# Both chunk pairs of a spatial mixing by one Strassen level, on eight fixed PSUM banks

## The chip, the core and the metric

The kernel runs on one core of a Trainium2 chip. The metric is the device time of one execution in microseconds, the median of several runs. TensorE (PE) does the matmuls, VectorE (DVE) and ScalarE (ACT) the elementwise work, GpSimd (POOL) a little of it. DMA transfers are started from the queues of SyncE (SP) and of ACT.

## The reference

```
xn = layernorm(x)                                  # x: 2048 x 512
# A: attention of 32 heads of width 16; each row sees itself and 7 earlier rows, 2 apart
q, k, v = split(xn @ wqkv)
s = softmax_window(q, k) @ v, then @ wo            # 512 x 512
# B: gated MLP with a mixing over the rows
z  = gelu(xn @ w_in)                               # 2048 x 1792
z1 = z[:, :896]
z2 = layernorm(z[:, 896:])
g  = w_sp @ z2 + b_sp[:, None]                     # w_sp: 2048 x 2048: the spatial mixing
return x + s * silu((z1 * g) @ w_out)              # w_out: 896 x 512
```

Everything is float32. The change is in the line of `g`.

## The kernel before

Every float32 operand of a matmul is written as the sum of a rounded high part and the rest. The helper `split` (L185, L186) makes them: ACT writes the high part, DVE subtracts it from the source and writes the low part. A product is then three matmuls (high x high, high x low, low x high), done by the helper `three` (L765 to L769, the line L767 in the profile). `prep` fetches a 128 x 512 block of weights by a DMA on SP's queue into one of four raw buffers and splits it into one of eight weight pairs.

The work goes through these stages on PE: `xn` and the product with `wqkv`; z1 (line L650 to L652), 7 blocks of 128 columns, kept transposed, gated later and until then in device memory (`z1_d`); z2 (L678 to L680), 16 row tiles in pairs (i, i + 8), then normalised and split into the large buffer `BIG`; the mixing (L767); the projection with `w_out` (tile `b`, L982 to L984); the product with `wo` (tile `s`, the same lines) and the end. The attention itself is DVE work with a share of POOL. It is emitted before z1 at the lowest priority and fills DVE from the z1 stage on; its results (`o_d`) are read by the product with `wo`.

The mixing forms g transposed: 7 column blocks f of z2, four chunks c of 512 rows each of the output, 16 row tiles s (8 upper, 8 lower) to sum over. z2 is the stationary operand, a 128 x 512 block of `w_sp` the moving one. Chunks 2 and 3 go plainly, one after the other: for each of 16 row tiles all 7 column blocks, in 7 PSUM banks. Chunks 0 and 1 go together by one level of Strassen's scheme over chunk (0 or 1), half of the rows (upper or lower) and half of the columns (f = 0 to 2, or 4 to 6; f = 3 is the odd column and goes plainly): seven products of 3 column blocks and 8 row tiles take the place of eight. The combinations that it needs are made ahead: `block_sums` loads two pairs of `w_sp` blocks, adds them in four DVE instructions (L639) and stores two 512 KB tiles to `sums_d`; `combine` (L712) does the same for z2 after its normalisation and stores to `t_d`. During the mixing `operand` loads those back (tile `tr`, L824) and splits them into parts of `BIG` that no product needs any more. `block_product` runs a product in four steps of two row tiles, and after each step does what its `steps` list says.

Results are multiplied with z1. Those of chunks 2 and 3 are stored to `g_d`, and loaded and split again by `late` when there is room in `BIG` (table `slots`); those of chunks 0 and 1 are split at once by `gated`.

Most temporary tiles of these stages are the eight wide buffers of the tag `t4` (128 x 1024): the z1 tiles before they are stored, the raw z2 tiles, the tiles of `block_sums` (`sa`, `sb`), the operands, the biases, the results between products. A tile takes a free buffer and holds it until its last reader is done.

The order of the instructions on each engine and of the DMA issues on SP and ACT is fixed when the kernel is built: a scheduler goes through the instructions by priority (program order, unless a priority is set by `urgent` or the attention's low one) and puts those first that are ready by its own estimate of time. The engines then work each in that order.

Of the kernel before, what the change touches and what calls it, by code (L numbers as in the profile page):

```python
# [57 lines left out]
def kernel(  # L58
# [67 lines left out]
    slots = {(0, f): f for f in range(4)}  # L126
    slots.update({(2, f): 4 + f for f in range(5)})
    slots.update({(1, f): 5 + f for f in range(4, FB)})
    slots.update({(2, 5): 12, (2, 6): 13, (0, 4): 18, (0, 5): 19, (0, 6): 22})
    slots.update({(3, 0): 23, (3, 1): 26, (3, 2): 27, (1, 0): 14, (1, 1): 15, (1, 2): 16, (1, 3): 17})  # L130
    slots.update({(3, 3): 20, (3, 4): 21, (3, 5): 24, (3, 6): 25})
# [497 lines left out]
    def block_sums(i):  # L629
        top, low = t4(f"sa_{i}"), t4(f"sb_{i}")  # L630
        nc.sync.dma_start(top, w_sp[0:2, i].rearrange("c p t -> p c t"))
        nc.sync.dma_start(low, w_sp[0:2, HT + i].rearrange("c p t -> p c t"))
        for out_, a, b in (
            (low[:, 1], top[:, 1], low[:, 1]),
            (top[:, 1], top[:, 0], top[:, 1]),
            (top[:, 0], top[:, 0], low[:, 1]),
            (low[:, 0], top[:, 0], low[:, 0]),
        ):
            nc.vector.tensor_tensor(out_, a, b, op=ALU.add)  # L639
        nc.scalar.dma_start(sums_d[0, i], top)  # L640
        nc.scalar.dma_start(sums_d[1, i], low)

    for f in range(FB):
# [18 lines left out]
        if f % 2:  # L662
            block_sums(f // 2)
# [33 lines left out]
    def z2_normal(j, zt):  # L697
# [6 lines left out]
    def combine(i, zts):  # L704
        b11, b12, b21, b22 = [z[:, p_] for z in zts for p_ in (first_part, last_part)]
        for out_, a, b, op in (
            (b11, b11, b12, ALU.subtract),
            (b12, b22, b12, ALU.subtract),
            (b22, b22, b11, ALU.add),
            (b21, b22, b21, ALU.subtract),  # L710
        ):
            nc.vector.tensor_tensor(out_, a, b, op=op)  # L712
        for a, zt in enumerate(zts):
            v = zt[:, first_part]
            src = bass.AP(
                tensor=v.tensor, offset=v.offset, ap=[list(v.ap[0]), [FH - F3, 2], [1, F3]]
            )
            nc.scalar.dma_start(t_d[a, i], src)

    early_pair = [wts.tile([P, CT], F32R, tag=f"w{n}", name=f"wsp_2_0{n}") for n in "hl"]  # L720
    split(*early_pair, fetch(w_sp[2, 0], CT, "wsp_2_0"))
    spatial = {(2, 0): early_pair}
    raw_z = {}
    for i in range(HT + 2):
        if i < HT:
            raw_z[i] = [t4(f"zt_{j}").rearrange("p i t -> p (i t)")[:, :FH] for j in (i, HT + i)]
            for h in range(2):
                for j, zt in zip((i, HT + i), raw_z[i]):
                    z2_half(j, h, zt)
                if i == HT - 1 and h == 0:  # L730
                    spatial[2, HT] = spatial_block(2, HT)
# [3 lines left out]
        if i > 1:  # L735
            for j, zt in zip((i - 2, HT + i - 2), raw_z[i - 2]):
                z2_normal(j, zt)
            combine(i - 2, raw_z[i - 2])

    def bias(c):  # L740
        t = t4(f"bb_{c}")
        nc.sync.dma_start(
            t, b_sp[c : c + 2, :].rearrange("c t -> (c t)").unsqueeze(0).to_broadcast([P, 2 * CT])
        )
        return t

    def load_o(g, k, i=None):
# [7 lines left out]
        else:  # L755
            oh, ol = half(2 * i), half(2 * i + 1)
# [22 lines left out]
    order = [i + h * HT for i in range(HT) for h in range(2)]  # L779
    bb = bias(2)  # L780
    banks = {(2, f): mm(f"g_2_{f}") for f in range(FB)}
    seeds = set()

    def seed(key, name, src, scale=1.0):
        banks[key] = mm(name)
        nc.scalar.activation(banks[key], src, AF.Copy, scale=scale)
        seeds.add(key)

    for c in (2, 3):
        for n, js in enumerate(order):  # L790
            w = spatial.get((c, js)) or spatial_block(c, js)
            for f in range(FB):
                key = c, f
                three(banks[key], z2_block(js, f), w, n == 0 and key not in seeds, n == NT - 1, key in seeds)
            if n == HT:
                if c == 2:
                    banks[3, 0] = mm("g_3_0")
                else:
                    b01 = bias(0)
                    seed(("p", 0), "p1_0", b01[:, 0])  # L800
            if c == 2 and n % 4 == 0 or c == 3 and n == 5:
                block_sums(3 + n // 4 if c == 2 else 7)
        for f0 in range(0, FB, 2):
            n = min(2, FB - f0)
            zl = z1_pair(c, f0, n)
            gts = None if (c, f0 + n - 1) in seeds and f0 else t4(f"gt_{c}_{f0}", n)
            for f in range(f0, f0 + n):
                zt, src = zl[:, f - f0], banks[c, f]
                if (c, f) not in seeds:
                    gt = gts[:, f - f0]  # L810
                    nc.vector.tensor_tensor(gt, src, bb[:, c - 2], op=ALU.add)
                    src = gt
                nc.vector.tensor_tensor(zt, src, zt, op=ALU.mult)
                if c == 2 and f < FB - 1:
                    seed((3, f + 1), f"g_3_{f + 1}", bb[:, 1])
                if c == 3 and f < 3:
                    key = ("p", f + 1) if f < 2 else ("o", 0)
                    seed(key, f"p1_{f + 1}", b01[:, 0])
            nc.scalar.dma_start(g_d[c - 2, f0 : f0 + n].rearrange("f p t -> p f t"), zl)

    def operand(i, half_, s0):
        raw = t4(f"tr_{half_}{i}_{s0}").rearrange("p i t -> p (i t)")[:, : 2 * F3]
        rv = raw.rearrange("p (j f t) -> p j f t", j=2, f=3)
        nc.sync.dma_start(  # L824
            rv, t_d[half_, s0 : s0 + 2, :, i].rearrange("j p (f t) -> p j f t", t=P)
        )
        hi, lo = [
            planes[:, FB - 3 :, s0 : s0 + 2, a].rearrange("p f j t -> p j f t") for a in range(2)
# [3 lines left out]
    def block_product(name, key, z, w, odd=None, start=True, steps=()):  # L832
        for n, s0 in enumerate(range(0, HT, 2)):
            pair_ = [(s, prep(w(s), CT, f"{name}_{s}")) for s in (s0, s0 + 1)]
            for f in range(3):
                for s, wp in pair_:
                    three(
                        banks[key, f], z(s, f), wp, start and s == 0, s == HT - 1, not start
                    )
            if odd:  # L840
                for s, wp in pair_:
                    three(banks["o", odd[0]], odd[1](s), wp, False, s == HT - 1, True)
            for do in steps[n] if steps else ():
                do()

    def upper(s, f):
        return z2_block(s, f)
# [240 lines left out]
```

## Time and profile before

| | |
|---|---|
| median of 3 runs | 708.12 us (708.11 to 708.29) |
| profiled execution | 708.39 us, span 706.6 us |
| PE busy | 700.8 us, 99% of the span |
| DVE busy | 586.4 us, 83% |
| ACT busy | 268.3 us, 38% |
| POOL busy | 112.6 us, 16% |
| DMA traffic | 159.29 MB, 225 GB/s in the mean |
| mixing on PE | 294.7 to 583.0 us |

The page of the profile shows one execution. A group of instructions is told by line, engine, operation and tiles; behind the bar stand its busy time, the mean duration of one in ns, the idle time of the engine just before them and what ended it. Matmuls overlap in the pipeline, so that the mean duration of one, some 390 ns, is longer than the distance to the next.

### The profile page before, as it was taken

What the parts mean: (1) busy time and instruction counts of PE and PEld (TensorE: products, weight loads), DVE (VectorE), ACT (ScalarE), POOL (GpSimd) and SP (SyncE); (2) the same over time, 40 slices, a digit from 0 to 9 for tenths busy, and PEclk for the clock granted to TensorE, in tenths of its full rate; (3) what the DMA queues carried; (4) which work ended last, traced back from release to release, by engine and by line L of the source; (5) the groups of instructions that cost most, each with busy time, mean ns of one, the idle gap of its engine ahead of it and who ended that gap; (6) DMA issues with size and microseconds to landing.
All of it is one profiled execution on the core that took longest, in us unless ns stands there. A gap on an engine that the chain in (4) does not pass through costs nothing.

```text
span 706.6 us, 9137 instructions
## 1 busy us (share of the span) xinstructions
PE 700.8 (99%) x3152; PEld 585.6 (83%) x3152; DVE 586.4 (83%) x845; ACT 268.3 (38%) x417; POOL 112.6 (16%) x110
## 2 busy tenths in 40 slices
PE   8999999999999999999999999999999999999997
PEld 7888888888888988888888888888888888888886
DVE  6774479999999899998999999999999989330464
ACT  4343332334442666662113111344545452131621
POOL 3100002211212344540121112111101100000000
PEclk9999999999999999999999999999999999999999
DMA  8768677778798132498969745878868682273785
GB/s 269 258 186 244 173 247 208 197 258 301 264 330 263 50 108 97 140 309 298 384 203 336 245 138 162 286 253 291 276 202 275 202 290 94 78 219 153 246 251 232
DMA packets 100110, 159.29 MB, mean 225 GB/s; under 512 B 9056, under 2 KB 51296, under 8 KB 100064
## 3 DMA queue, kind: packets, MB, share of 16 engines
q1 hardware_dynamic: 61424, 116.11, 51.1%
q10 hardware_dynamic: 38640, 42.60, 17.4%
q8 instruction: 24, 0.39, 0.2%
q14 instruction: 22, 0.18, 0.1%
HBM read 107.74 MB, written 50.94 MB: 225 GB/s over the span
## 4 chain that ended last, share of the span: by engine, by line
PE 98%; DMA 1%; DVE 1%; SPq 0%; issue 0%
PE g L767 22%; PE q L767 12%; PE p L767 6%; PE qkv L373 6%; PE qkv L375 6%; PE qkv L374 6%; PE z L680 4%; PE z L679 4%; PE z L678 4%; PE z L652 4%; PE b L983 4%; PE z L650 4%; PE b L984 4%; PE b L982 4%; PE z L651 4%; PE s L983 2%
## 5 line engine op out<-in xcount | busy, mean ns | idle before, releaser
L571 POOL TENSOR_TENSOR pv<-pv 128x1024 f32<-128x1024 f32 x29 | 69.8, 2406 | 377.1 <-DVE pv L561 377.0
L517 DVE TENSOR_TENSOR pr<-k,q 128x2048 f32<-128x2048 f32 x32 | 73.2, 2287 | 6.6 <-DMA q<-qkv_d 4.6
L561 DVE TENSOR_TENSOR pv<-v,lg 128x2048 f32<-128x2048 f32 x32 | 73.2, 2288 | 0.6
L524 DVE TENSOR_REDUCE lg<-pr 128x128 f32<-128x2048 f32 x32 | 72.9, 2277 | 0.0
L390 ACT ACTIVATE stage<-qkv 128x512 f32<-128x512 f32 x36 | 21.5, 596 | 47.6 <-PE qkv L375 47.6
L993 ACT ACTIVATE bt<-b 128x512 f32<-128x512 f32 x16 | 9.5, 597 | 45.6 <-PE b L984 45.6
L699 ACT ACTIVATE zt<-zt,nmz,mvz 128x896 f32<-128x896 f32 x16 | 17.8, 1134 | 20.8 <-POOL nmz L695 20.8
L680 PE MATMUL z<-w_0h,BIG 128*128 128x512 f32 x64 | 25.0, 391 | 0.0
L679 PE MATMUL z<-w_0l,BIG 128*128 128x512 f32 x64 | 25.0, 391 | 0.0
L678 PE MATMUL z<-w_0h,BIG 128*128 128x512 f32 x64 | 24.9, 389 | 0.0
L186 DVE TENSOR_TENSOR o_1l<-ol,o_1h 128x512 fp32r<-128x512 f32 x3 | 2.1, 689 | 26.7 <-ACT o_1h L185 26.7
L1037 DVE TENSOR_TENSOR sg<-s,sg 128x512 f32<-128x512 f32 (+1 forms) x17 | 11.2, 659 | 15.1 <-PE s L984 15.0
L269 DVE TENSOR_TENSOR xT<-xT,mr 128x512 f32<-128x512 f32 x20 | 13.7, 687 | 11.3 <-DMA mr<-mv_d 6.7
L576 DVE TENSOR_TENSOR pv<-pv 128x512 f32<-128x512 f32 x32 | 21.8, 682 | 0.1
L680 PE MATMUL z<-w_1h,BIG 128*128 128x384 f32 x64 | 21.5, 336 | 0.0
L678 PE MATMUL z<-w_1h,BIG 128*128 128x384 f32 x64 | 21.5, 335 | 0.0
L679 PE MATMUL z<-w_1l,BIG 128*128 128x384 f32 x64 | 21.4, 335 | 0.0
L690 DVE BATCH_NORM_STATS2 zst<-zt 128x6 f32<-128x448 f32 x32 | 18.8, 605 | 2.4 <-ACT zt L681 2.2
L659 ACT ACTIVATE z1t<-z 128x512 f32<-128x512 f32 x21 | 12.4, 593 | 20.2 <-PE z L652 17.1
L186 DVE TENSOR_TENSOR BIG<-zt,BIG 128x896 fp32r<-128x896 f32 x16 | 17.3, 1089 | 0.6 <-ACT BIG L185 0.4
L375 PE MATMUL qkv<-wqkv_0h,BIG 128*128 128x512 f32 x43 | 16.7, 389 | 0.0
L373 PE MATMUL qkv<-wqkv_1h,BIG 128*128 128x512 f32 x43 | 16.7, 389 | 0.0
(543 smaller groups left out, 2185.0 us busy)
## 6 DMA issues: line engine op xcount, KB each, us to landing
qkv_d<-stage ACTq DMA_DIRECT2D x24, 512.0 KB
k<-qkv_d SPq DMA_DIRECT2D x16, 704.0 KB
v<-qkv_d SPq DMA_DIRECT2D x16, 704.0 KB
z_d<-z1t ACTq DMA_DIRECT2D x14, 512.0 KB
t_d<-zt ACTq DMA_DIRECT2D x16, 384.0 KB
zl<-z_d SPq DMA_DIRECT2D x12, 512.0 KB
tr<-t_d SPq DMA_DIRECT2D x16, 384.0 KB
x<-in_x SPq DMA_DIRECT2D x16, 256.0 KB
```

The lines of the kernel that those rows point to most:

```text
L373: nc.tensor.matmul(pq, xh[:, k], wh, start=k == 0, stop=False)
L374: nc.tensor.matmul(pq, xh[:, k], wl, start=False, stop=False)
L375: nc.tensor.matmul(pq, xl[:, k], wh, start=False, stop=k == KB - 1)
L517: line(nc.vector.tensor_tensor(pr, taps(ks[u], j0), qb.unsqueeze(1).to_broadcast([P, W, NJ * CS]), op=ALU.mult))
L524: line(nc.vector.tensor_reduce(lgs[u][:, :, j0 * HS : (j0 + NJ) * HS], pr.rearrange("p w (i d) -> p w i d", d=DH), axis=AX.X, op=ALU.add,))
L561: line(nc.vector.tensor_tensor(pv.rearrange("p w (i d) -> p w i d", d=DH), taps(vs[u], j0).rearrange("p w (i d) -> p w i d", d=DH), lgs[u] ...
L571: eng.tensor_tensor(pv[:, 0:4], pv[:, 0:4], pv[:, 4:8], op=ALU.add)
L678: nc.tensor.matmul(pz, xh[:, k], wh, start=k == 0, stop=False)
L679: nc.tensor.matmul(pz, xh[:, k], wl, start=False, stop=False)
L680: nc.tensor.matmul(pz, xl[:, k], wh, start=False, stop=k == KB - 1)
L767: nc.tensor.matmul(pg, z[a], w[b], start=start and i == 0, stop=stop and i == 2, skip_group_check=seeded)
L983: nc.tensor.matmul(pp[:, cols], hi, wl, start=False, stop=False)
```

## The change

Chunks 2 and 3 go by the same scheme as chunks 0 and 1. The two pairs are called a = 0 (chunks 0 and 1) and a = 1 (chunks 2 and 3). The products of the pairs alternate: m1, m2, m6, m7, m4, m5, m3, each for a = 0 and then for a = 1. Each pair has four fixed PSUM banks, three for the column blocks of the running product and one for the odd column. They are allocated once; ACT writes a bias or an earlier product into them (`seed`) where the next product is to be added to it. The banks of the second pair are first written by four matmuls with the first weights, and then seeded (`second_seeds`).

`block_sums` is done for both pairs: seven blocks of the first pair in the z1 stage (three before), the eighth and all eight of the second pair in the first two products of the mixing. The first product of each pair is copied out of PSUM and stored to `x_d` (`kept`), to be loaded and subtracted later (`stored_gates`); the sum after the third product goes to `y_d` (`spill`) and is loaded by `upper_last`. `combine` forms its differences with the other sign, and one of the four results is split at once into `BIG`, so that three are stored, not four. Only the first four results of chunks 0 and 2 go through `g_d`. The order of the chunks in the projection with `w_out` is 1, 3, 0, 2 instead of 2, 0, 3, 1, and in the product with `wo` 1, 3, 0, 2 instead of 0, 2, 3, 1.

```diff
-    g_d = dram.tile([2, FB, P, CT], F32, name="g_d")
-    sums_d = dram.tile([2, HT, P, 2, CT], F32, name="sums_d")
-    t_d = dram.tile([2, HT, P, 2, F3], F32, name="t_d")
+    g_d = dram.tile([2, ODD + 1, P, CT], F32, name="g_d")
+    x_d = dram.tile([2, ODD, P, CT], F32, name="x_d")
+    y_d = dram.tile([2, ODD, P, CT], F32, name="y_d")
+    sums_d = dram.tile([2, 2, HT, P, 2, CT], F32, name="sums_d")
+    t_d = dram.tile([3, HT, P, F3], F32, name="t_d")
...
-        if f % 2:
-            block_sums(f // 2)
+        block_sums(0, f)
...
-        split(zh, zl, blocks(zt, FB))
+        split(zh[:, :n], zl[:, :n], blocks(zt, FB)[:, :n])
...
+        split(*[t[:, ODD + 1 :] for t in z2_at(i)], blocks(b22, ODD))
...
+        nc.scalar.dma_start(t_d[:2, i].rearrange("a p t -> p a t"), src)
+        nc.scalar.dma_start(t_d[2, i], b21)
...
+    b_a = t4("b_a")
+    nc.sync.dma_start(
+        b_a, b_sp[0:2, :].rearrange("c t -> (c t)").unsqueeze(0).to_broadcast([P, 2 * CT])
+    )
+    biases = [[b_a[:, 0], b_a[:, 1]]]
...
-    for c in (2, 3):
-        for n, js in enumerate(order):
-            w = spatial.get((c, js)) or spatial_block(c, js)
-            for f in range(FB):
-                key = c, f
-                three(banks[key], z2_block(js, f), w, n == 0 and key not in seeds, n == NT - 1, key in seeds)
...
+    banks = {}
+    for n in range(8):
+        a, f = n // 2 % 2, n // 4 * 2 + n % 2
+        banks[a, f] = mm(f"g_{a}_{f}")
+
+    def seed(a, f, src, scale=1.0):
+        nc.scalar.activation(banks[a, f], src, AF.Copy, scale=scale)
+
+    def evict(a, f, out_):
+        nc.scalar.activation(out_, banks[a, f], AF.Copy)
+
+    def block_product(a, name, z, w, odd=None, start=False, stop=False, steps=()):
+        for n, s0 in enumerate(range(0, HT, 2)):
+            pair_ = [(s, w(s)) for s in (s0, s0 + 1)]
+            for f in range(ODD):
+                for s, wp in pair_:
+                    three(banks[a, f], z(s, f), wp, start and s == 0, s == HT - 1, not start)
+            if odd:
+                for s, wp in pair_:
+                    three(banks[a, ODD], odd(s), wp, False, s == HT - 1, True)
+            for do in steps[n] if steps else ():
+                do()
...
+    def stored_gates(a, f0):
+        zl = z1_pair(2 * a, f0, 2)
+        n = min(2, ODD - f0)
+        xl = t4(f"xl_{a}_{f0}", n)
+        nc.sync.dma_start(xl, x_d[a, f0 : f0 + n].rearrange("f p t -> p f t"))
...
+            times(zl[:, f - f0], banks[a, f], zl[:, f - f0])
+            if f < ODD:
+                seed(a, f, xl[:, f - f0], -1.0)
+        nc.scalar.dma_start(g_d[a, f0 : f0 + 2].rearrange("f p t -> p f t"), zl)
...
+    def spill(a):
+        ta, tb = t4(f"ya_{a}"), t4(f"yb_{a}", 1)
+        for f in range(ODD):
+            y = ta[:, f] if f < 2 else tb[:, 0]
+            evict(a, f, y)
+            nc.vector.tensor_tensor(banks[a, f], banks[a, f], biases[a][1], op=ALU.add)
...
+        seed(a, ODD, biases[a][1])
...
+    def second_seeds():
+        biases.append([wts.tile([P, CT], F32, tag=f"w{n}", name=f"b_b{n}") for n in "hl"])
...
+            nc.tensor.matmul(
+                banks[1, f], z2_block(0, 0)[0], early_pair[0], start=True, stop=True
+            )
+        for f in range(ODD + 1):
+            seed(1, f, biases[1][0])
...
+        0, "m1a", at(0, 0), plain(0, 0, 0), odd(0),
+        steps=([second_seeds, sums(0, 7)], [sums(1, 0)], [sums(1, 1)], [sums(1, 2)]),
...
+        1, "m1b", at(0, 0), plain(1, 0, 0), odd(0),
+        steps=([sums(1, 3)], [sums(1, 4)], [sums(1, 5), sums(1, 6)], [sums(1, 7)]),
...
+    kept(1)
...
+        0, "m2a", at(1, 0), plain(0, 0, 1), odd(1),
...
+    block_product(1, "m2b", at(1, 0), plain(1, 0, 1), odd(1))
...
+        0, "m6a", at(0, LAST), summed(0, 0, 0), steps=([T4[0]], [T4[1]], [T4[2]], [T4[3]])
...
+    spill(0)
+    block_product(1, "m6b", at(0, LAST), summed(1, 0, 0))
+    spill(1)
```

The products m7 (with the odd column), m4 (with the odd column), m5 and m3 follow in the same manner. `summed` reads its weights from `sums_d`, `plain` from `w_sp`.

More of the change, by code (lines that the diff above doesn't have):

```diff
@@ L755, in load_o @@
         else:
[L756 removed]
+            oh, ol = i
         arrived[g] = split(
@@ L827, in operand @@
         hi, lo = [
-            planes[:, FB - 3 :, s0 : s0 + 2, a].rearrange("p f j t -> p j f t") for a in range(2)
+            planes[:, f0 : f0 + ODD, r0 + s0 : r0 + s0 + 2, b].rearrange("p f j t -> p j f t")
+            for b in range(2)
         ]
         split(hi, lo, rv)
[L832 to L844, printed above, removed]
@@ new lines, in upper_last, with sums @@
+    def upper_last(a, f0, n):
+        zl, yl = z1_pair(2 * a, LAST + f0, n), t4(f"yl_{a}_{f0}", n)
+        nc.sync.dma_start(yl, y_d[a, f0 : f0 + n].rearrange("f p t -> p f t"))
+        for f in range(f0, f0 + n):
+            minus(yl[:, f - f0], banks[a, f], yl[:, f - f0])
+            gated(2 * a, LAST + f, yl[:, f - f0], zl[:, f - f0])
+    T1, T3, T4 = [[later(operand, i, s0) for s0 in range(0, HT, 2)] for i in range(3)]
+    def sums(a, i):
+        return later(block_sums, a, i)
+    with urgent(300):
+        for f in range(ODD + 1):
+            seed(0, f, biases[0][0])
@@ L977, in proj @@
+    wout = [prep(w_out[:, f, :], D, f"wout_{f}") for f in range(FB)]
+    upper_last(1, 0, 2)
+    upper_last(1, 2, 1)
+    for a in range(2):
+        late(a, 0, 2)
+        late(a, 2, 1)
     def proj(n, src, w, name, cols=slice(0, D)):
```

303 lines of the change are left out of this document (126 added, 177 removed).

## The prediction

> **What bounds the kernel now.** I read the page first: the busy shares (busy us, share of the span, instructions) and the chain that ended last.
>
> ```profile
> PE 700.8 (99%) x3152; PEld 585.6 (83%) x3152; DVE 586.4 (83%) x845; ACT 268.3 (38%) x417; POOL 112.6 (16%) x110
> PE 98%; DMA 1%; DVE 1%; SPq 0%; issue 0%
> ```
>
> PE is the bound: nothing but fewer PE instructions can shorten this, and every wait that PE gets is paid in full. Then the chain in order of time (start, length, what), for the mixing, and PE's timeline at the two ends of what follows it.
>
> ```profile
> 294.83 152.36 PE g L767 x672
> 447.19 43.52 PE p L767 x192
> 490.71 20.40 PE q L767 x90
> ...
> 581.83 1.36 PE o L767 x6
> ```
> ```profile
> 583.03 0.39 PE L982 MATMUL b<-wout_0h,BIG 128*128 128x512 f32 x1
> ...
> 659.19 0.39 PE L982 MATMUL s<-BIG 128*128 128x512 f32 x1
> ```
>
> The plain pair is 672 matmuls in 152.36 us without a gap, 0.2267 us each. All the mixing, 672 + 600 = 1272 matmuls, is 288.4 us, from 294.7 to 583.03; then the projection b (336 matmuls, 76.2 us) and, from 659.19, s.
>
> Last, windows: what the other engines have to spare. Columns: stretch, its length, busy us of each engine, granted clock, share of DMA time, GB/s.
>
> ```profile
> 141.30:217.40 76.10, 76.10 (x338) 63.00 (x337) 74.11 (x93) 30.89 (x48) 15.03 (x7) 1.00 0.84 282
> 217.40:294.80 77.40, 77.40 (x386) 69.62 (x385) 74.60 (x117) 47.39 (x66) 33.43 (x52) 1.00 0.37 119
> 294.80:403.00 108.20, 108.20 (x479) 89.56 (x478) 105.17 (x159) 30.68 (x47) 22.48 (x22) 1.00 0.86 296
> 583.20:659.40 76.20, 76.20 (x337) 63.09 (x337) 30.44 (x43) 20.91 (x34) 0.00 (x0) 1.00 0.38 130
> 335.00:340.00 5.00, 5.00 (x23) 4.14 (x23) 3.82 (x6) 2.04 (x3) 0.00 (x0) 1.00 1.05 402
> 350.00:355.00 5.00, 5.00 (x23) 4.13 (x22) 4.96 (x9) 0.63 (x1) 0.00 (x0) 1.00 1.02 404
> 105.00:603.00 498.00, 498.00 (x2242) 417.84 (x2241) 484.38 (x676) 199.08 (x308) 102.64 (x93) 1.00 0.70 230
> ```
>
> DVE is full from 105 to 603 us (484.38 of 498.00), because the attention fills what the rest leaves. The DMA is at 0.86 in the first 108 us of the mixing; where its share is full it moves 402 to 404 GB/s. Between them lies the risk.
>
> **PE's share of the change.** A Strassen pair is seven products of 72 matmuls plus 24 for the odd column in four of them: 600 instead of 672. The second pair saves 72; four opening matmuls of the second pair's banks are added. Net 68 x 0.2267 = 15.4 us. Alternating the pairs moves matmuls and adds none.
>
> **DVE.** Its instructions follow each other closer than their durations say; starts give the pitch.
>
> ```profile
> 560.08 0.69 DVE L186 TENSOR_TENSOR q_3l<-q_3r,q_3h 128x512 fp32r<-128x512 f32 x1
> 560.68 0.96 DVE L186 TENSOR_TENSOR BIG<-tr,BIG 128x768 fp32r<-128x768 f32 x1
> 561.55 0.69 DVE L186 TENSOR_TENSOR q_4l<-q_4r,q_4h 128x512 fp32r<-128x512 f32 x1
> ```
> ```profile
> L186 DVE TENSOR_TENSOR BIG<-zt,BIG 128x896 fp32r<-128x896 f32 x16 | 17.3, 1089 | 0.6 <-ACT BIG L185 0.4
> L712 DVE TENSOR_TENSOR zt<-zt 128x384 f32<-128x384 f32 x16 | 8.5, 534 | 0.0
> ```
>
> So 0.60 us for 512 columns, 0.87 for 768, and with the same 0.09 off the durations 1.00 for 896 and 0.45 for 384. Added: sums of the second pair, 8 x 4 x 0.60 = 19.2; weight splits, 112 instead of 88, 24 x 0.60 = 14.4. z2 splits: eight of 512, 896 and 384 each instead of sixteen of 896, 16.4 against 16.0, +0.4. Removed: operand splits, 12 instead of 16, 4 x 0.87 = 3.5; gating, seeds' adds and late splits, 78 instead of 81, 1.8. Net +28.7 us. That is on the path only if the attention ends too late.
>
> ```profile
> 605.38 0.45 DVE L584 STREAM_TRANSPOSE tt<-pv 128x256 f32<-128x256 f32 x1
> 617.71 0.69 DVE L186 TENSOR_TENSOR BIG<-wo_0r,BIG 128x512 fp32r<-128x512 f32 x1 [11.87 <-ACT BIG L185]
> ```
> ```profile
> 618.42 12.51 SPq L750 DMA_DIRECT2D ol<-o_d  x18
> ```
>
> The attention ended at 605.8; with a DVE that is as full as before it ends at 634.5. PE then leaves b at 659.2 - 15.4 = 643.8, and only the second row group of s (another 48 matmuls, 654.7) needs the last attention unit, whose loads and splits took about 10 us here. Spare: 654.7 - 10 - 634.5 = 10 us. Cost taken 0, hidden by b, whose 76.2 us hold 30.44 us of DVE now; without that cover 28.7 - 10 = 19 us.
>
> **ACT and the queues.** ACT gains 24 weight splits and some 15 seeds and evictions, 39 x about 0.6 = 23 us, in a mixing where it is busy 30.68 of 108.20 us: 0. An eviction between two products of one pair runs under the other pair's product, at least 72 x 0.2267 = 16.3 us, while four copies are 2.4 us: 0. SP gets 16 loads of the sums, 24 weight fetches, and x and y loads, less 6 of operands and gates. It issues in order, so a sums load that waits for one of the eight wide buffers holds the weight fetches behind it; PE waits once the eight weight pairs (about 2.3 us of work each) are used up, some 18 us.
>
> **DMA.** Sizes by the list of issues (queue, count, KB each):
>
> ```profile
> sa<-in_w_sp SPq DMA_DIRECT2D x8, 512.0 KB
> sums_d<-sa ACTq DMA_DIRECT2D x8, 512.0 KB
> q_0r<-sums_d SPq DMA_DIRECT2D x4, 256.0 KB
> tr<-t_d SPq DMA_DIRECT2D x16, 384.0 KB
> k<-qkv_d SPq DMA_DIRECT2D x16, 704.0 KB
> q<-qkv_d SPq DMA_DIRECT2D x16, 256.0 KB
> ```
>
> One block of sums is four transfers of 0.524 MB, 2.1 MB. Before, five blocks fell into the mixing, spread over its first 105 us; now nine are asked for in its first two products (44 us), and the last eight must be there for the second pair's third product, which ends at 528 x 0.2267 = 119.7 us. Up to then: sums 9 x 2.1 = 18.9 MB; weight blocks, 6 x 8 less some 4 fetched earlier and 8 read ahead, 52 x 0.262 = 13.6; kept products out and back 12 x 0.262 = 3.1, the next ones out 1.6; gates (z1 in, result out) 16 x 0.262 = 4.2; first operands 1.6; the end of the z2 stores and the biases about 3.2: 46.2 MB, and 48.2 with one attention unit (k, v, q and its results, 1.97). At 404 GB/s that is 119.3 us: just in time. At the mean of the stretch 294.80:403.00 (296 GB/s at 0.86, so 344 at full share) it is 140.1 us, 20.4 us too long. Cover: the first pair's next product, 96 x 0.2267 = 21.8 us, needs no sums of the second pair, and PE's order can be changed, as these rows show (first weights again after the ninth):
>
> ```profile
> 307.86 0.39 PE L767 MATMUL g<-wsp_9l,BIG 128*128 128x512 f32 x1
> 308.08 0.39 PE L767 MATMUL g<-wsp_0h,BIG 128*128 128x512 f32 x1
> ```
>
> Ends of the price: 0, and 20.4 without cover. The full-share rows are nearest, being themselves a time of sums traffic; I take a fifth of the way, 4 us, for what the order and the buffers waste. Below 0 is excluded: more bytes free nothing. The Trainium skill's page "DMA: Bandwidth & Descriptors", section "Where 436 GB/s comes from", holds that traffic between HBM and SBUF is bound at about 358 GB/s by the core's share of HBM. By that, as an estimate, 48.2 MB would be 14.9 us too long and the sum 708. The trace disagrees: 402 and 404 GB/s over 5 us.
>
> In the z1 stage four more blocks of sums, 8.4 MB or 20.8 us at 404, meet 0.16 x 76.1 = 12 us of free DMA; the other 9 us fit into the z2 stage, free to 0.63. Cost 0; without that cover 9.
>
> **Start of the mixing.**
>
> ```profile
> 305.48 0.60 ACT L681 ACTIVATE zt<-z 128x512 f32<-128x512 f32 x1 [1.15 <-DMA t_d<-zt]
> ```
> ```profile
> 311.54 1.04 DVE L186 TENSOR_TENSOR BIG<-zt,BIG 128x896 fp32r<-128x896 f32 x1
> ```
>
> The last z2 rows wait for wide buffers held by stores, and the bank of this one becomes the first pair's odd bank, due 18 matmuls (4.1 us) after 294.7. The upper row 7 is split at 311.5, done at 17.9 us after the start; the first product needs it after 72 matmuls, 16.3 us. The early bias takes an eighth buffer more. Ends: 0 if PE takes other products' matmuls meanwhile, about 10.8 - 4.1 = 7 us for the bank, and 15 if row 7 also slips as far as that row did. Taken 0: PE had the same bank late here and lost nothing.
>
> **Sum.** The profiled execution took 708.39 us (span 706.6), 0.27 above the median of the runs, 708.12. 708.39 - 15.42 + 4 = 696.97, so 697.
>
> **Rivals.**
> - DMA bound. The sums of the second pair come too late, and the weight fetches stand behind them on SP, so the cover doesn't hold either. Place: the second pair's third product; price 20.4 us, 708.4 - 15.4 + 20.4 = 713, slower, with two more attention units in that time (3.9 MB at 344 GB/s, 11.4 us) 725; it decides once the uncovered wait passes 15.4 us. For it: a DMA share of 0.86 now, and nine blocks of sums asked for in 44 us. Against: the full-share rates, and that PE has no wait so far. Chance 0.25; 0.03 of it is the case of the page's rule, 708.
> - Late banks and rows at the start of the mixing: 7 to 15 us lost, 700 to 708. For: the buffer wait quoted. Against: PE passed it before. 0.08.
> - The attention ends late. DMA waits open 25 us more of idle time on DVE, s then waits 15: 708; with 30, 713. 0.06.
> - The change doesn't pay in full: the extra sums in the z1 stage hold wide buffers that the gelus need, 9 us: 702 to 706. 0.04.
>
> **How the numbers follow.** My forecast, waits mostly covered, 692.5 to 706.7, has 0.57. A measurement tells about 0.2% (1.4 us) from no change. Faster: 0.57 + 0.04 (z1) + 0.05 of the late start = 0.66. Same: 0.03 + 0.02 (late start) + 0.02 (attention) = 0.07. Slower: 0.22 + 0.01 + 0.04 = 0.27. The range goes from 691.5 (nothing lost, 693, and a tail that ends a little otherwise) up into the DMA case, to 718; some 0.14 lies above, 0.03 below.
>
> **What would show it.** Right: PE at 3084 instructions, busy about 685 us; the mixing 273 us plus waits; these under weight splits or seeds in the stretch 90 to 120 us after the mixing's start; DMA share near 1.0 in its first 100 us; the last attention transpose near 635 us. Wrong: PE gaps over 15 us in all, waiting for weight splits whose sums came late; the s stage starting with a wait for attention loads; or PE gaps before 294 us.

## The result and the profile after

The changed kernel takes 740.59 us (median of 4 runs, 738.82 to 743.27), the kernel before 708.12 beside it: a ratio of 1.046, 95% interval 1.043 to 1.049. It is slower by 32.5 us, where 11 us of gain were forecast. The profiled execution took 738.82 us, its span is 737.0.

The page: busy us, share of the span and instructions; the granted clock in 40 slices; the chain that ended last.

```profile
PE 694.2 (94%) x3084; PEld 576.9 (78%) x3084; DVE 611.9 (83%) x902; ACT 284.5 (39%) x458; POOL 115.2 (16%) x110
PEclk9999999999999999998987789999999999999999
DMA packets 109952, 182.37 MB, mean 247 GB/s; under 512 B 10064, under 2 KB 50256, under 8 KB 109904
PE 69%; DVE 14%; DMA 8%; issue 4%; ACT 3%; POOL 2%; SPq 1%; ACTq 0%; DVEq 0%
```

The 68 matmuls are gone (3152 to 3084), but PE is no longer the bound all the way: its share fell from 99% to 94%, and 23 MB more are moved. Who PE waited for (us in total, times, longest):

```profile
PE g L771 <- ACT xa L792: 17.7, 2, 10.6
PE g L771 <- ACT g L789: 15.4, 1, 15.4
PE g L771 <- ACT wsp_12h L191: 2.4, 1, 2.4
PE g L917 <- ACT zt L686: 1.2, 1, 1.2
PE g L771 <- DVE wsp_12l L192: 0.5, 1, 0.5
```

Sum 37.2 us, nearly all of it three waits: two for the copies out of PSUM (`kept`, tile `xa`), one for a seed (`stored_gates`). The mixing runs from 294.5 to 613.4, 318.9 us, where 1204 matmuls need 273.0: 45.9 us lost. The windows over it (stretch, length, busy us of PE, weight load, DVE, ACT, POOL, clock, DMA share, GB/s):

```profile
294.80:305.00 10.20, 9.04 (x40) 7.00 (x39) 10.20 (x18) 9.22 (x16) 2.08 (x4) 1.00 0.49 138
305.00:320.00 15.00, 14.84 (x67) 11.96 (x65) 14.54 (x23) 10.61 (x17) 6.61 (x9) 1.00 0.72 241
320.00:340.00 20.00, 20.00 (x88) 16.54 (x89) 19.44 (x34) 7.09 (x12) 0.00 (x0) 1.00 0.98 337
340.00:360.00 20.00, 12.88 (x50) 10.18 (x49) 19.82 (x29) 6.24 (x11) 3.68 (x2) 0.83 1.03 388
380.00:400.00 20.00, 9.39 (x30) 7.04 (x30) 19.93 (x26) 1.97 (x4) 2.35 (x1) 0.68 1.01 381
400.00:427.00 27.00, 11.60 (x51) 9.35 (x50) 26.90 (x36) 9.53 (x16) 4.76 (x2) 0.75 0.98 342
426.50:430.00 3.50, 3.48 (x8) 2.81 (x9) 3.50 (x8) 1.55 (x3) 0.00 (x0) 0.50 0.79 232
320.00:427.00 107.00, 71.02 (x285) 56.38 (x286) 106.09 (x151) 28.18 (x48) 14.21 (x6) 0.84 1.00 363
```

The transfers are full from 320 to 427 us, at 363 GB/s in the mean, but not in the first 25 us of the mixing (shares of 0.49 and 0.72). The row from 426.5 us shows a second, smaller loss: right after a long wait PE runs at half its clock. PE's timeline at the longest wait, and then after two shorter ones:

```profile
426.52 0.80 PE L771 MATMUL g<-ws_0h,BIG 128*128 128x512 f32 x1 [15.40 <-ACT g L789]
427.11 0.63 PE L771 MATMUL g<-ws_0l,BIG 128*128 128x512 f32 x1
427.54 0.63 PE L771 MATMUL g<-ws_0h,BIG 128*128 128x512 f32 x1
...
430.44 0.40 PE L771 MATMUL g<-ws_3h,BIG 128*128 128x512 f32 x1
430.68 0.40 PE L771 MATMUL g<-ws_3l,BIG 128*128 128x512 f32 x1
```
```profile
377.08 0.50 PE L771 MATMUL g<-wsp_12h,BIG 128*128 128x512 f32 x1 [2.35 <-ACT wsp_12h L191]
378.07 0.50 PE L771 MATMUL g<-wsp_12l,BIG 128*128 128x512 f32 x1 [0.49 <-DVE wsp_12l L192]
...
380.91 0.63 PE L771 MATMUL g<-wsp_15h,BIG 128*128 128x512 f32 x1
381.34 0.63 PE L771 MATMUL g<-wsp_15l,BIG 128*128 128x512 f32 x1
```

Starts are 0.43 us apart until 430.4, then 0.23: some 1.6 to 1.9 us lost after each long wait, 5.2 after the three of them. From 379.5 to 381.8, after the two shorter waits, the starts are as far apart, 1.3 us more. Together that is 6.5 of the 8.7 us by which the loss exceeds the waits; the rest lies in gaps too small for the list. The Trainium skill's page "TensorE: Matmul & The Clock Gate", Part 1 (the HAM clock gate), says that about 3.4 us without work put the clock back to half, that it takes about 3.4 us of work to return, and that matmuls of 512 columns then start 426.7 ns apart; the rows after the long waits agree (0.43 us apart, for 3.4 to 3.9 us). The rows after the shorter waits do not agree with the 3.4 us without work: here 2.35 and 0.49 us, with 0.5 us of work between them, were enough.

A seed overwrites a bank, so it stands behind VectorE's product of that bank with z1 (L836), and that product behind a load of z1 (tile `zl`). SyncE issued the first of these loads as late as 408.74. By its semaphore's records in the trace it had landed by 415.8; the product began only at 425.15, since VectorE's order put attention and weight splits before it, without a gap:

```profile
408.74 0.46 SPq L780 DMA_DIRECT2D zl<-z_d  x1
```
```profile
421.48 2.28 DVE L523 TENSOR_TENSOR pr<-k,q 128x2048 f32<-128x2048 f32 x1
...
425.15 1.27 DVE L836 TENSOR_TENSOR zl<-g,zl 128x512 f32<-128x512 f32 x2
```
```profile
425.86 1.20 ACT L789 ACTIVATE g<-xl 128x512 f32<-128x512 f32 x2 [6.73 <-DVE zl L836]
```

The first pair's copies stood in ScalarE's fixed order behind splits of weights that landed late, and the second pair's waited for the store of a sum to give a wide buffer free:

```profile
343.85 0.63 ACT L191 ACTIVATE wsp_13h<-wsp_13r 128x512 fp32r<-128x512 f32 x1 [5.16 <-DMA wsp_13r<-in_w_sp]
347.66 1.06 ACT L792 ACTIVATE xa<-g 128x512 f32<-128x512 f32 x2
...
392.35 1.09 ACT L792 ACTIVATE xa<-g 128x512 f32<-128x512 f32 x2 [10.48 <-DMA sums_d<-sa]
```

### The profile page after: what moved, and what is told of

Same layout as the page of the kernel before. It is cut to its first block, busy times and chain, and to the rows that moved or that the text cites. A ratio compares the mean times of both kernels' runs of the same rounds, so it can differ in the third digit from the quotient of the medians.

```text
span 737.0 us, 9252 instructions
## 1 busy us (share of the span) xinstructions
PE 694.2 (94%) x3084; PEld 576.9 (78%) x3084; DVE 611.9 (83%) x902; ACT 284.5 (39%) x458; POOL 115.2 (16%) x110
## 4 chain that ended last, share of the span: by engine, by line
PE 69%; DVE 14%; DMA 8%; issue 4%; ACT 3%; POOL 2%; SPq 1%; ACTq 0%; DVEq 0%
PE g L771 26%; PE qkv L380 5%; PE qkv L381 5%; PE qkv L379 5%; PE b L1002 3%; PE b L1001 3%; PE b L1000 3%; PE z L658 3%; PE z L657 3%; PE z L656 3%; PE s L1002 2%; PE s L1001 2%; PE s L1000 2%; DMA o_d<-tt 2%; DVE pr L523 2%
## 5 line engine op out<-in xcount | busy, mean ns | idle before, releaser
L771 PE MATMUL g<-ws_0h,BIG 128*128 128x512 f32 x52 | 19.9, 401 | 15.4 <-ACT g L789 15.4
L771 PE MATMUL g<-wsp_8h,BIG 128*128 128x512 f32 x32 | 13.7, 429 | 17.7 <-ACT xa L792 17.7
L645 DVE TENSOR_TENSOR sb<-sa,sb 128x512 f32<-128x512 f32 x32 | 22.9, 727 | 3.0 <-DMA sb<-in_w_sp 2.5
L771 PEld LDWEIGHTS g<-ws_0h,BIG 128*128 128x128 f32 x52 | 10.0, 192 | 17.9 <-ACT g L789 15.8
L771 PEld LDWEIGHTS g<-wsp_8h,BIG 128*128 128x128 f32 x32 | 6.5, 203 | 20.2 <-ACT xa L792 18.9
```

Of the source, the lines that this page charges most:

```text
L771: nc.tensor.matmul(pg, z[a], w[b], start=start and i == 0, stop=stop and i == 2, skip_group_check=seeded)
```

## The experiments

The theory to begin with was **bytes**: the second pair's sums (16.8 MB loaded and stored) fill the transfers, and all that PE needs comes late. Its rivals: VectorE's 32 additions; ScalarE's order; the wide buffers that the sums hold. Where no interval is given, a time is one run, beside a run of the kernel before of 708 to 710; the changed kernel's own runs spread over 4.5 us, so that differences under some 4 us are not told apart.

### Which part of the sums costs it

**Without the second pair's sums**

```diff
-        return later(block_sums, a, i)
+        return later(block_sums, a, i) if a == 0 else (lambda: None)
...
```

> The eight blocks of sums of the second pair are left out (their products read the first pair's sums instead, so this part of the result is another). Both theories, buffers and bytes: PE's waits in the mixing fall from 37 us to under 6 and the time to 692 to 702 us. A third, that the alternating products or their copies cost PE something whatever the sums do: above 715 us.

696.65 us. PE had one wait of 0.9 us in the mixing. The whole loss comes from these sums, 740.6 - 696.65 = 44 us. The rest of the change does nearly what the sum said: 12.2 us under the kernel before (708.81 beside it) of the 15.4 that the matmuls are worth. Of the other 3.2 us some 2 were lost ahead of the mixing, which began at 296.6 here, and 1.5 in it.

**Without their stores**

```diff
-        nc.scalar.dma_start(sums_d[a, 0, i], top)
-        nc.scalar.dma_start(sums_d[a, 1, i], low)
+        if a == 0:
+            nc.scalar.dma_start(sums_d[a, 0, i], top)
+            nc.scalar.dma_start(sums_d[a, 1, i], low)
...
```

> The second pair's sums are loaded and added, but not stored (8.4 MB less to move, and ACT issues no stores that wait for them; the products read the first pair's sums). Theory buffers: a wide buffer is held for less long, about half, 700 to 715 us. Theory bytes: half of the extra bytes are gone, 715 to 725 us. If loads alone fill the buffers: 725 us or more.

720.65 us: 20 of the 44 us are gone with half the bytes. As bytes had it, but a store also holds its buffer and a place in ScalarE's order.

**Without their additions**

```diff
-            nc.vector.tensor_tensor(out_, p_, q_, op=ALU.add)
+            if a == 0:
+                nc.vector.tensor_tensor(out_, p_, q_, op=ALU.add)
```

> The 32 additions of the second pair's block sums are left out (so its sums are plain blocks); their loads, their stores and the buffers that they hold stay. Theory bytes (the loads and stores of these sums fill the transfer engines between 320 and 427 us): DMA share there still about 1.0, PE's waits in the mixing still 30 to 40 us, time 733 to 743. Rival VectorE (the sums come late because their 32 x 0.65 = 21 us of additions stand in VectorE's queue behind the attention): the waits fall to under 15 us and the time to under 720. An attention that ends some 20 us earlier is expected by both.

745.28 us, no gain, and a little above the 733 to 743 of the theory of bytes. VectorE was no longer full, and PE waited all the same:

```profile
320.00:427.00 107.00, 75.55 (x291) 58.53 (x289) 85.74 (x114) 28.79 (x49) 14.25 (x6) 0.84 0.98 344
```

So VectorE's work for the sums is not it.

**Stores from SyncE**

```diff
-        nc.scalar.dma_start(sums_d[a, 0, i], top)
-        nc.scalar.dma_start(sums_d[a, 1, i], low)
+        q = nc.sync if a else nc.scalar
+        q.dma_start(sums_d[a, 0, i], top)
+        q.dma_start(sums_d[a, 1, i], low)
```

> The 16 stores of the second pair's sums are issued by SyncE and no longer by ScalarE; bytes, additions and buffers stay. Theory bytes: nothing that counts, 733 to 745. Rival by ScalarE's queue (the copies, seeds and weight splits stand in ScalarE's order behind stores that wait for VectorE): ScalarE's waits in the mixing go, PE's waits fall by half or more, under 722. SyncE's loads now stand behind the stores' waits, which could also make it longer than 745.

743.31 us: nor is it on which queue the stores are issued.

**The copies out of the wide buffers**

```diff
-        ta, tb = t4(f"xa_{a}"), t4(f"xb_{a}", 1)
+        k0, k1 = weight_pair(f"xk_{a}_0"), weight_pair(f"xk_{a}_1")
...
```

> The copies of the first products go into four weight buffers instead of wide ones; all sums as before. Theory buffers (the copies wait for wide buffers that the sums hold): the two waits for the copies, 7.1 and 10.6 us, go, together with some 5 us of slow clock behind them: 715 to 725 us. Theory bytes (the DMA is full, so any order waits as long): the wait moves to weights or seeds, 735 to 745 us.

741.89 us. The waits for the copies vanished, and one for a seed took their place:

```profile
PE g L771 <- ACT g L789: 32.4, 1, 32.4
```

A wait that is taken away at one place comes back at the next: the copies were where the lateness showed, not its source.

**The sums spread over four products**

```diff
-        steps=([sums(1, 3)], [sums(1, 4)], [sums(1, 5), sums(1, 6)], [sums(1, 7)]),
+        steps=([sums(1, 1)], [], [sums(1, 2)], []),
...
```

(in the second product; the first keeps `sums(1, 0)`, the third and fourth take the rest)

> The second pair's sums stand in the steps of the first four products of the mixing instead of the first two. If it is their early place in the program: 715 to 725 us. If the scheduler starts their loads whenever a wide buffer is free, whatever their place: 735 to 745 us, as the changed kernel. Theory bytes: 730 to 745 us.

742.35 us. The full stretch only became longer (share 0.92 to 1.02 from 320 to 460 us), and the seeds waited there instead.

**Without a part of the attention's loads**

```diff
+            if 9 <= u <= 12:
+                ks[u], qs[u] = ks[8], qs[8]
+                return
...
```

(and the same for `vs`, units 8 to 11)

> The loads of k, q and v of four of the attention's sixteen units are left out (the units that load between 317 and 427 us compute with the tiles of the unit before them); all else stays, the second pair's sums too. It leaves out 4 x 1.66 = 6.7 MB of what the transfers move in the full stretch. Theory bytes, whosever they are: 6.7 MB at 380 GB/s are 17.5 us, time 718 to 726. Theory that only the sums' own buffers and places in the queues count: the attention's loads do not matter, 735 to 742.

728.8 us, 11.8 less for 6.7 MB: less than bytes forecast, but others' bytes count as well. 1.8 us a MB would make 30 of the 44 us out of 16.8 MB, not all.

**The same bytes without buffers**

```diff
+                    ins = nc.sync.dma_start(
+                        spare_d[k, r, i].rearrange("p c t -> c p t"), w_sp[2:4, r * HT + i]
+                    )
...
```

> The second pair's block sums are left out (its summed products read the first pair's); in their places stand copies from device memory to device memory of as many bytes as the sums' loads and stores carried, 32 of 512 KB, issued by SyncE behind the weights of the same step. They hold no buffer in SBUF, nothing waits for them, VectorE and ScalarE do nothing for them. Theory bytes: the transfers are full again between 300 and 420 us, the weights and gates come late, 722 to 745. Rival by buffers (what cost the time were the wide buffers that the sums held, and the order in which they were given out): 695 to 705, as without the sums.

1015.08 us, and nothing learnt on the question. The copies ran alone and slowly; windows of this run:

```profile
295.00:320.00 25.00, 13.26 (x56) 9.83 (x54) 12.46 (x21) 8.13 (x15) 2.08 (x4) 0.86 0.13 49
320.00:340.00 20.00, 0.00 (x0) 0.00 (x0) 0.00 (x0) 0.00 (x0) 0.00 (x0) 0.50 0.15 60
```

A share of 0.13 is two of sixteen engines. The Trainium skill's page "DMA: Bandwidth & Descriptors", section "Why a DMA increments its semaphore by 16 and not by 1", says that a transfer is dealt to as many engines, up to 16, as divide its slowest dimension; I had written the copies with a slowest dimension of 2. The rows agree.

### Can the sums be made elsewhere

Between 235 and 295 us, in the z2 stage, the changed kernel moved 90 to 129 GB/s at a share of 0.26 to 0.38. Six versions tried to use that room, or to do without the sums; the diffs show where the sums went.

**Five in the z2 stage, in the raw buffers**

```diff
+        if 2 <= i < 2 + 5:
+            raw_sums(1, i - 2)
...
```

(`raw_sums` is `block_sums` on four tiles of the pool `raw` instead of two wide ones)

> Everything is computed. Five of the second pair's eight block sums are made in the z2 stage, in the four small raw buffers that lie idle there, where the transfers' share was 0.33, 0.38 and 0.26 between 235 and 295 us; the last three stay in the second product of the mixing. Theory bytes: 5/8 of 16.8 MB, 10.5 MB, leave the stretch that was full, some 27 us of transfer at 385 GB/s; PE's waits in the mixing fall from 37 us to under 8, and the time to 695 to 706, below that of the kernel before. Rival by the order of ScalarE's queue (first products' copies and seeds stand behind the stores of the sums): it would gain as well, since five eighths of those stores leave too, but as much is left as three sums give, 10 us or more, 712 to 722. Rival z2 (the transfers only move the shortage there): PE idle between 235 and 295 us, 10 us or more.

756.07 us, worse. One wait, of another kind:

```profile
PE g L793 <- ACT wsp_1h L191: 46.3, 1, 46.3
```

In VectorE's order the additions of a sum stood some 2 to 9 us apart, with others' work between them, so that the four of each of the first four sums took 12 to 18 us; the fifth sum still held the raw buffers at 345 us, and the mixing's weights need those.

**Three in raw buffers**

```diff
+        if 1 <= i < 1 + 3:
+            raw_sums(1, i - 1)
...
```

> Everything is computed. Three of the second pair's block sums are made in the z2 stage in the four small raw buffers (the transfers' share there was 0.26 to 0.38 from 235 us on), five stay in the first two products. Theory bytes: 6.3 MB, 16 us at 385 GB/s, leave the full stretch; of the 37 us of waits 15 to 25 are left, 718 to 730, and the mixing starts within 3 us of 294.5. Rival by place and not by bytes (each sum costs some time in whatever stage it is made): 735 or more.

736.78 us: little gain, as the rival by place had it (735 or more). But the mixing's first weights came late again (9.44 of 15 us busy from 295 to 310), and five sums still filled the stretch behind, so that the run does not decide for it.

**Three in raw buffers, two in wide ones**

```diff
+        if i in (2, 4):
+            block_sums(1, 2 + i // 2)
...
```

> Everything is computed. Five of the second pair's block sums are made in the z2 stage: three in the raw buffers, and two in two wide buffers, one of which is free there because the bias rows are loaded later; three stay in the first two products. Theory bytes: 10.5 MB leave the full stretch; what is left there (about 40 MB in 104 us from the rates without these sums, 31 MB, and 6.3 MB) is near what the transfers carry, waits under 10 us, 700 to 712. Rival by place: 735 or more. If the z2 stage cannot take them, PE idles before 300 us by what they are late.

731.21 us, between the two forecasts. Its windows tell two things:

```profile
295.00:325.00 30.00, 12.35 (x41) 9.03 (x40) 30.00 (x52) 18.66 (x29) 13.95 (x24) 0.66 0.66 213
325.00:427.00 102.00, 97.97 (x431) 80.44 (x429) 95.55 (x137) 40.39 (x68) 13.17 (x7) 1.00 0.96 342
```

From 325 to 427 us, with three sums instead of eight, PE worked 98 of 102 us although the transfers were at 0.96: a full road alone does not stop PE. But 17.7 us were lost before, where the last gelus of z2 came late: ScalarE had waited ahead of two of them 7.86 us for the split of an earlier row, and 4.12 us for the store of one of the two sums.

**Four in raw buffers, added on GpSimd, with and without a fifth in wide ones**

```diff
-            nc.vector.tensor_tensor(out_, p_, q_, op=ALU.add)
+            nc.gpsimd.tensor_tensor(out_, p_, q_, op=ALU.add)
...
```

> Everything is computed. Five of the second pair's sums in the z2 stage: four in the raw buffers with their additions on GpSimd (16% busy, so they need not stand among VectorE's operations, where they were 4 to 9 us apart), one in two wide buffers early in the stage; three in the first two products, which the run with five in the z2 stage bore from 325 to 427 us without a wait. Theory of a full road: the mixing starts within 3 us of 294.5, waits under 10 us, 698 to 710. Rival: the wide buffers of the one sum, or GpSimd's additions before the small operations that scale the rows, hold up the z2 stage again, PE idle before 300 us, 712 to 735.

> Everything is computed. As the run with five, without the one sum in wide buffers: four sums in the z2 stage in the raw buffers on GpSimd, four in the first two products. Theory of a full road: four more sums just fit behind 294 us, 700 to 712. Rival, a price for each sum left there: 715 to 722.

732.16 and 723.26 us. The fifth sum in wide buffers made PE wait 8.9 us in the z2 stage, against 2.5; without it the best complete version came out, still 15 us behind the kernel before: the mixing's start lost some 5 us, and four sums behind it most of the rest. Both theories of the last run miss, the rival by 1 us.

**Added when used**

```diff
+            if half_ == 0:
+                t = pair_in("sf_" + n, w_sp[2:4, s].rearrange("c p t -> p c t"))
...
+            plus(t, t[:, 1])
...
```

> Everything is computed. The second pair's block sums are not made ahead: each weight is added from its plain blocks when its product comes (three blocks and a stored sum in the second pair's first summed product, two in each of the other three). Of the 16.8 MB that these sums moved before 427 us nothing is left there; the bytes come back spread from about 400 us on, 17 MB loaded in place of 8.4 and 2.1 stored, 4.2 MB of it in the second pair's first summed product of 16.3 us. Additions of the second pair: 40 in place of 32, 5 us more of VectorE, the attention to end at about 640. Theory bytes: PE's waits before 420 us under 3, as without the sums (696.65); the second pair's first summed product asks 6.3 MB loaded and 2.1 stored, about 22 us of transfer at 385 GB/s in 16.3, so 2 to 8 us may be waited there: 697 to 706. Rival (any 25 MB more on the second pair's way cost the same wherever they lie): 720 or more. Rival VectorE (the additions on the way to the weights stand behind the attention's 2.3 us operations): many waits under these weights' splits, 710 to 725.

740.50 us (738.74 to 741.22; ratio to before 1.045, 1.043 to 1.048). Up to 400 us PE had no wait over 0.9 us. Then the weights' loads and additions themselves were late:

```profile
PE g L771 <- ACT ws_0h L191: 23.8, 3, 11.6
PE g L771 <- DVE ws_0l L192: 5.9, 3, 2.5
```

The rival VectorE of its expectation: the first additions stood behind 4.5 us of attention, after loads issued 2.3 us before the product was due.

### Bytes or buffers

**Half of the sums**

```diff
+        return later(block_sums, a, i) if a == 0 or i % 2 == 0 else (lambda: None)
...
```

> Four of the second pair's eight block sums are left out (its summed products read the first pair's for every other block); the other four stay at their places in the first two products. Theory of a full road: without these sums the transfers move 31 MB in the 104 us from 294 us on, and could move 40 at 385 GB/s; four sums are 8.4 MB and just fit, 697 to 706. Theory of a price for each sum, (740.6 - 696.65) / 8 = 5.5 us, from buffers and places in the queues: 715 to 722.

709.82 us, between the two forecasts: four sums cost 13 us, and four more another 31. The price isn't the same for each, and no step from nothing to all either.

**A quarter of the bytes, and almost none**

```diff
+        n = CT // 4 if a else CT
+        top, low = top[:, :, :n], low[:, :, :n]
...
```

(with 4 in place of `CT // 4` in the second)

> The second pair's eight block sums are made on the first quarter of each block's columns only, and its summed products read the first pair's sums, so three quarters of them are left out: the same 16 loads, 32 additions and 16 stores, in the same wide buffers, with the same waits, at the same places of the queues, but 4.2 MB in place of 16.8. Theory bytes: as with four sums or fewer, 697 to 710. Rival by buffers and queues (the sums take the wide buffers that the gates' loads and the copies need, and their stores stand ahead in ScalarE's order): 720 or more, with the waits under the seeds and copies as before.

> As the run with a quarter of the columns, but with four of 512: the same loads, additions, stores and wide buffers of the second pair's sums, with 0.13 MB in place of 16.8; nearly all of these sums is left out, and the summed products of the second pair read the first pair's. Theory bytes alone: 695 to 700, as without the sums. Theory that the wide buffers or the places in the queues carry the other half: 708 to 718, with waits under the copies and seeds of the first two products.

718.00 and 714.30 us. Both forecasts of bytes alone miss (the rival's 720 in the first run too, by 2): with 1% of the bytes 17.7 us of the 44 remain.

**Almost none, in buffers of their own**

```diff
+            own = const.tile([P, 2, 2, 4], F32, tag="own", name=f"so_{a}_{i}", bufs=2)
+            top, low = own[:, 0], own[:, 1]
...
```

> As the run with four columns, but the second pair's sums lie in two small buffers of their own and hold no wide one; their loads wait for a weight split of the same step, so that they keep about their places. The same number of loads, additions and stores; nearly all of the second pair's sums is left out. Theory wide buffers: 695 to 702. Theory places in the queues: as the run with four columns in wide buffers, within 3 us. Theory bytes alone: both 695 to 700.

702.59 us: between the two theories, nearer to wide buffers (11.7 of the 17.7 us gone). The waits of the two runs, first with four columns in wide buffers, then in their own:

```profile
PE g L773 <- DVE ws_2l L192: 5.5, 1, 5.5
PE g L773 <- ACT xa L794: 4.7, 2, 4.5
PE g L773 <- ACT ws_1h L191: 1.7, 1, 1.7
```
```profile
PE g L780 <- DVE ws_6l L193: 2.1, 1, 2.1
PE g L926 <- ACT zt L695: 1.7, 1, 1.7
PE g L780 <- ACT ws_0h L191: 1.0, 1, 1.0
```

The place is only in part the expected one: in wide buffers the longest wait is for weights of a summed product, not for copies or seeds.

What the buffers do is seen in when SyncE issued the first load for the gates, in four runs: four columns in wide buffers, in their own, a quarter in wide ones, no sums:

```profile
381.30 0.46 SPq L782 DMA_DIRECT2D zl<-z_d  x1
```
```profile
353.39 0.38 SPq L789 DMA_DIRECT2D zl<-z_d  x1
```
```profile
387.84 0.46 SPq L782 DMA_DIRECT2D zl<-z_d  x1
```
```profile
347.89 0.38 SPq L780 DMA_DIRECT2D zl<-z_d  x1
```

The gates' loads need wide buffers too. They come at 348 us where the sums leave those alone, at 381 where the sums hold them even without bytes, and at 409 in the changed kernel. In the run with own buffers the sums also stand at other places in SyncE's order, from 295 to 378 us instead of 317 to 370, so that it does not part the buffers from that order. The order is fixed when the kernel is built: the sums, emitted earlier, are given the buffers that come free, and the gates' loads are put behind them in SyncE's order. That the bytes themselves lengthen the hold of a buffer is not shown: the store that the second pair's copies waited for took 5.6 us to land in the changed kernel (386.72 to 392.33), and with four columns it took as long, from its issue to the start of the copies:

```profile
368.29 0.52 ACTq L648 DMA_DIRECT2D sums_d<-sa  x1
...
373.78 1.09 ACT L794 ACTIVATE xa<-g 128x512 f32<-128x512 f32 x2 [4.29 <-DMA sums_d<-sa]
```

So the 44 us are, by what was taken away in this order: **bytes 26** (740.6 to 714.3), **wide buffers 12** (to 702.6), **the sums' instructions and their places in the queues 6** (to 696.65). By the time lost in the mixing alone (its length less 273.0 us: 45.9, 21.2, 9.1 and 1.5) they are 25, 12 and 8. The parts may work on each other, so another order of taking away could share them out otherwise; the last one is near the spread of single runs.

What stays open: whether a version that gives the gates' loads their buffers first, and makes four sums in the z2 stage, gets below 708. No complete version did.

## Why the prediction was wrong, point by point

- **PE's share** (15.4 us): right: 3084 instructions, and without the sums 12.2 us came out of it. PE's busy time was to be 685 us and is 694.2: matmuls at half the clock count as busy for longer, and without the sums it is 685.8.
- **DVE** (28.7 us more, the attention to end at 634.5): right. Its busy time rose by 25.5, and the last transpose of the attention ended at 636.4. Its cover, the product b, was not put to the test: PE left it at 690, 46 us later than forecast.

```profile
635.94 0.45 DVE L590 STREAM_TRANSPOSE tt<-pv 128x256 f32<-128x256 f32 x1
```

- **The z1 stage, the start of the mixing** (0 each): right; the mixing started at 294.5, and its start lost 1.5 us. These covers hold only as long as the stages aren't given more: the versions with sums in the z2 stage lost 5 to 46 us there.
- **ACT and the queues** (0): wrong. The step compared ACT's busy time with its idle time, and a copy's 2.4 us with a product's 16.3. But ACT works in a fixed order: it had 28 us of work between 320 and 427 us, and was late all the same, since copies and seeds, or what stood ahead of them in its order, waited for transfers, buffers and VectorE.
- **DMA** (4 us, ends 0 and 20.4): this is the step that failed, in four places. The rate: it took the transfers as full from the first moment and near 404 GB/s. They moved 138 and then 241 GB/s in the first 25 us, and 363 over the 107 us after; at 363 the ledger's 48.2 MB take 133 us, 13 too long and not 4. The attention: the ledger counted one unit, 1.97 MB, and three were loaded by its date, a fourth from 416 us on; the attention is last in priority, but a load that is ready goes ahead. The date: there was one, the end of the second pair's third product at 119.7 us, though that product's first sums are due at its start, 456 x 0.2267 = 103.4, and all bytes before it counted as alike. The three long waits ended at 54, 98.5 and 132 us and stood before the second product of each pair and the first pair's third, all ahead of the product that the ledger dated: what PE waited for was not sums but copies and seeds, and ahead of these stood late weights, the store of a sum, a late load for the gates and VectorE's order. The cover, the first pair's next product, could not be used: it adds into the same banks as the first pair's third product, and that was the one that waited.
- **The upper end of the price** (20.4 us) was a shortage of bytes at the stretch's mean rate. Measured, the sums cost 44 us, of which bytes took 26; the 18 for buffers and places had no term. The one sentence on the wide buffers priced only weight fetches held up on SyncE, and let the weight pairs cover them; the gates' loads and the copies, which want the same buffers, were not in it.
- **The clock** after a wait had no term either: each long wait costs 1.6 to 1.9 us more than its length, and the two shorter ones at 377 us cost 1.3 more.
- **The rivals**: the DMA rival (0.25, 713 to 725) had a part of the cause (bytes, 26 of the 44 us), not the place, nor the size; no wait of the list is for a split of summed weights, its sign. The rule of the Trainium skill's page "DMA: Bandwidth & Descriptors", section "Where 436 GB/s comes from" (358 GB/s, 708), isn't what decided: the transfers moved 381 to 388 GB/s over 20 us, though 363 over the whole 107, and the waits came before its date.

## What to carry to other kernels

Where a fixed pool of buffers serves several users, a term for bytes is not enough: ask who takes the next free buffer, who stands behind him in a queue whose order was fixed before the run, and which of these PE needs first. A ledger of bytes needs a date for each consumer, and a small transfer with an early date can count most. And a change that leaves PE the bound at 99% pays every new wait in full, with a surcharge for the clock, so a gain of 2% is soon lost: here three waits took twice as much.

## What the runs showed of the hardware that was not expected

- The transfers carried 337 to 388 GB/s over stretches of 20 to 27 us at a share of 0.98 or more, 363 over the whole 107 us, below the 402 to 404 of the 5 us stretches on which the prediction leaned.
- With the transfers at a share of 0.96 for 102 us PE lost only 4 us, and at 0.76 with four columns in wide buffers it lost 7 of 104. The share tells where the road is full, not whether anybody waits:

```profile
294.60:398.60 104.00, 97.09 (x416) 78.23 (x415) 92.76 (x161) 47.35 (x79) 19.79 (x17) 0.98 0.76 232
```
